# Window attention and top-1 experts on one core: maxima in PSUM, small routing operations on GpSimd, ranks and the early table first in a step, late casts

## The chip, the cores and the metric

The kernel runs on one core of a Trainium2 chip. The core has TensorE (matmuls, into PSUM), VectorE, ScalarE and GpSimd, which work from queues of their own and meet through semaphores, and DMA queues, here those of SyncE and of GpSimd. The metric is the device time of one execution in microseconds (us).

## What is computed

Eight heads of causal attention with a window of 64 over 8 sequences of 576 tokens, and then a mixture of 8 experts in which each token goes to the one expert with the largest logit, weighted by its softmax share. All in float32.

```python
scores = scale * np.matmul(q, k.transpose(0, 1, 3, 2))          # 8 x 8 x 576 x 64
mask = (rel >= 0) & (rel < 64)
scores = np.where(mask, scores, -1e9)
attn = softmax(scores); x = (attn @ v)                           # to 4608 rows of 512
expert_idx = np.argmax(x @ w_gate, axis=1); gate_w = their softmax share
out[mask_e] = gate_w * (np.maximum(x[mask_e] @ w1[e], 0) @ w2[e])   # e = 0..7, F = 1024
```

## The kernel before

**Steps.** The loop at L766 runs 36 attention steps of 128 tokens (NS = 36) and 7 more to drain. A step i is a software pipeline, and the order in which the code calls its parts is the order in each engine's queue: nothing reorders it later. `exps(i-1)` (ScalarE, eight activations `pf`), `evac(i-2)` (ScalarE, `tsb`), `apart(i-2)` (GpSimd, two products `pm` with the mask, L403), `cols_t` (ScalarE, `xT`, L441), then `scores(i)` (TensorE, into `s_b`), `folded` and `largest` (VectorE: fold of the two halves of the window, maximum `mx`, scaled negative maximum `mxs`, L379), `values(i-3)` (TensorE, into `x_b`), one routing matmul (`fast`), `rows_t(i-4)` (TensorE transposes into `m_b` or `t_b`), `transp(i-1)` (TensorE), `shares(i-3)` (VectorE: `den`, `rs`, `xrow`, and the store of the rows by SyncE), and at its end what routing has queued. `scores` alternate between two buffers until step 29 (TURN) and share one from then on. `x_b` also holds the small routing results (`rest_b`) beside the values.

**Routing.** Tokens are routed in four rounds of 8, 6, 12 and 10 tiles. A round's steps s1 to s8 (L489 to L554) go through the queue `slow`, three a step: maxima of logits `lm`, `ld`, `eq`, the exponentials `ex` (L498, ScalarE), the choice `oh`; s4 in the following step (the ranks within each expert: TensorE matmuls with `tri` and `ones`, and ScalarE's copy `rks`, L513), then `pos`, `se`, `g`, `fl`, `mid`, and the parts of the gate in the next. `puts` (L809, four a step) write a one-hot row for each tile (`hot_row`), and after rounds 1 and 2 the tables for two early experts each (`early_parts`, `early_table`, `early_rows`: TensorE gathers, VectorE makes indices `eidx` and gates, GpSimd fetches the tokens `xg`).

**Early experts.** From step 29 the generator `early` (`first_passes`) runs the passes of experts 0 to 3 in pieces between the steps' parts (`forward`, six pieces a step), and after the steps alone. The tokens of expert 0 are transposed in steps 27 and 28 (`turn`, into `m_b`, before the scores). Weights come as float32 and are split in a high part `whi` (ScalarE, L220) and a rest `wlo` (VectorE, L221); `split_ahead` makes one such pair a step from step 29 on, at the step's end, and loads the next by SyncE's queue.

**The plan.** After the steps, `plan` (L636) works out the blocks of the remaining passes on VectorE, a few small operations for every second piece of `early`, and ends in one matmul that spreads `blk` (`diag`, L699); then the table for all later passes, and the passes (`chain`), which fill the time from about 290 us.

## Time and profile before

| | |
|---|---|
| median of 3 runs | 691.14 us (688.66 to 693.12) |
| the profiled execution | 692.4 us, span 690.6 us |
| TensorE busy | 627.2 us, 91% |
| VectorE busy | 424.7 us, 61% |
| ScalarE busy | 359.4 us, 52% |
| GpSimd busy | 193.4 us, 28% |

The span runs from the first to the last instruction of the program. Busy times are those of one engine's instructions; shares over the span mix the attention steps (to about 146 us), the steps with expert pieces between (to about 230 us), the early experts and the plan (to about 290 us) and the later passes. Where an instruction waits, the rows name what ended the idle time.

### The profile page before, as it was taken

To read this page: it belongs to the slowest core of one execution; us is meant where nothing else is said; L and a number is where in the kernel's file an instruction comes from. 1 tells how busy PE (TensorE), PEld (TensorE's weight loads), DVE (VectorE), ACT (ScalarE), POOL (GpSimd) and SP (SyncE) were. 2 spreads that over 40 slices of the span, in tenths; PEclk is the share of its full clock that TensorE was granted. 3 is DMA by queue.
4 is the path that set the end of the run, shared out by engine and by line. 5 is a ranking of instruction groups with operands and counts; after the bars stand their busy time and mean duration, and the time that the engine had idled before them with its cause. 6 is when DMAs were issued, how large, how long until landed. Compare 5 with 4: busy or idle time off the path is not lost.

```text
span 690.6 us, 17098 instructions
## 1 busy us (share of the span) xinstructions
PE 627.2 (91%) x7002; PEld 552.4 (80%) x7002; DVE 424.7 (61%) x817; ACT 359.4 (52%) x760; POOL 193.4 (28%) x159
## 2 busy tenths in 40 slices
PE   5797778678889979999999999999999999999995
PEld 4676666566768768889999999999999999999994
DVE  4687989655676877564544555555565556555651
ACT  4566555644454333553444656555555565555551
POOL 4565545633235103411111212122212212110111
PEclk9999998998999989999999999999999999999999
DMA  9887775854223635854444666666566667555520
GB/s 318 295 261 263 237 280 190 265 182 148 93 88 123 267 122 174 290 206 165 148 168 153 221 216 204 218 227 222 209 219 223 224 217 239 202 193 195 214 92 32
DMA packets 34247, 138.14 MB, mean 200 GB/s; under 512 B 4844, under 2 KB 5996, under 8 KB 24432
## 3 DMA queue, kind: packets, MB, share of 16 engines
q1 hardware_dynamic: 27760, 118.08, 49.3%
q0 software_dynamic: 6400, 18.88, 8.0%
q8 instruction: 57, 0.93, 0.5%
q14 instruction: 30, 0.25, 0.1%
HBM read 119.11 MB, written 19.92 MB: 201 GB/s over the span
## 4 chain that ended last, share of the span: by engine, by line
PE 69%; DVE 14%; ACT 7%; issue 6%; DMA 2%; POOL 0%; DVEq 0%; ACTq 0%; POOLq 0%
PE m_b L279 16%; PE s_b L243 14%; PE t_b L279 13%; PE x_b L243 13%; PE x_b L417 3%; ACT pf L387 3%; PE s_b L361 3%; PE s_b L180 2%; DMA raw<-wall 2%; DVE wlo L221 2%; DVE mx L376 2%; DVE s_b L372 2%; ACT whi L220 2%; DVE mxs L379 1%; DVE xrow L427 1%
## 5 line engine op out<-in xcount | busy, mean ns | idle before, releaser
L221 DVE TENSOR_TENSOR wlo<-raw,whi 128x1024 fp32r<-128x1024 f32 (+1 forms) x158 | 187.2, 1185 | 172.3 <-ACT whi L220 167.9
L220 ACT CAST whi<-raw 128x1024 fp32r<-128x1024 f32 (+1 forms) x158 | 160.9, 1020 | 102.1 <-PE s_b L243 51.1
L403 POOL TENSOR_TENSOR pm<-tsb,cs 128x512 f32<-128x512 f32 x72 | 93.8, 1324 | 109.5 <-ACT tsb L396 106.7
L251 POOL DMA_INDIRECT out<-ys,idx_sb x32 | 40.9, 1277 | 182.9 <-ACT ys L250 178.0
L387 ACT ACTIVATE pf<-s_b,mxs 128x64 f32<-128x64 f32 x288 | 62.7, 333 | 47.8 <-DVE den L423 32.9
L169 POOL DMA_INDIRECT xg<-xs,idx_sb x32 | 34.5, 1080 | 153.4 <-PE s_b L180 140.4
L243 PE MATMUL s_b<-whi,hh 128*128 128x512 f32 x176 | 71.1, 404 | 0.0
L243 PE MATMUL s_b<-whi,hl 128*128 128x512 f32 x176 | 70.1, 398 | 0.6 <-DVE hl L286 0.6
L279 PE MATMUL t_b<-xh,whi 128*128 128x256 f32 (+1 forms) x240 | 70.6, 294 | 0.0
L279 PE MATMUL m_b<-xh,whi 128*128 128x256 f32 (+1 forms) x240 | 70.5, 294 | 0.0
L243 PE MATMUL s_b<-wlo,hh 128*128 128x512 f32 x176 | 70.1, 398 | 0.0
L279 PE MATMUL t_b<-xh,wlo 128*128 128x256 f32 (+1 forms) x240 | 69.7, 291 | 0.0
L279 PE MATMUL m_b<-xh,wlo 128*128 128x256 f32 (+1 forms) x240 | 69.7, 290 | 0.0
L279 PE MATMUL m_b<-xl,whi 128*128 128x256 f32 (+1 forms) x240 | 69.4, 289 | 0.2 <-DVE xl L183 0.2
L279 PE MATMUL t_b<-xl,whi 128*128 128x256 f32 (+1 forms) x240 | 69.4, 289 | 0.0
L285 ACT ACTIVATE hh<-m_b 128x256 fp32r<-128x256 f32 (+1 forms) x82 | 32.5, 397 | 62.0 <-PE m_b L279 61.9
L417 PE MATMUL x_b<-ring,pm 64*64 64x65 f32 x2176 | 47.3, 233 | 16.2 <-issue 6.9
L417 PEld LDWEIGHTS x_b<-ring,pm 64*64 64x64 f32 x2176 | 42.7, 145 | 22.2 <-issue 17.7
L243 PE MATMUL x_b<-wlo,hh 128*128 128x512 f32 x144 | 56.7, 393 | 0.0
L243 PE MATMUL x_b<-whi,hh 128*128 128x512 f32 x144 | 56.5, 393 | 0.0
L243 PE MATMUL x_b<-whi,hl 128*128 128x512 f32 x144 | 56.5, 392 | 0.0
L361 PE MATMUL s_b<-ring 64*64 64x128 f32 x1024 | 43.9, 294 | 8.9 <-ACT pf L387 8.4
(177 smaller groups left out, 1273.7 us busy)
## 6 DMA issues: line engine op xcount, KB each, us to landing
raw<-wall SPq DMA_DIRECT2D x76, 1024.0 KB, 5.0
ring<-qkv SPq DMA_DIRECT2D x66, 386.0 KB, 4.3
xs<-xrow SPq DMA_DIRECT2D x36, 256.0 KB, 2.2
ring<-qkv SPq DMA_DIRECT2D x4, 256.0 KB, 5.2
ring<-qkv SPq DMA_DIRECT2D x4, 130.0 KB, 4.9
ring<-qkv SPq DMA_DIRECT2D x1, 512.0 KB
xg<-xs,idx_sb POOLq DMA_INDIRECT x32, 4.1
out<-ys,idx_sb POOLq DMA_INDIRECT x32, 2.8
```

The costliest lines, as they stand in the source:

```text
L169: nc.gpsimd.indirect_dma_start(out=t[:, u], out_offset=None, in_=xs[0:rows], in_offset=bass.IndirectOffsetOnAxis(ap=ix, axis=0), bounds_ch ...
L180: nc.tensor.transpose(xp[:, kk], t[:, u, kk * P:(kk + 1) * P], ident)
L220: nc.scalar.copy(out=hi[:, s], in_=raw[:, s])
L221: nc.vector.tensor_tensor(out=lo[:, s], in0=raw[:, s], in1=hi[:, s], op=ALU.subtract)
L243: nc.tensor.matmul(y, lhsT=x[:, us], rhs=w[:, C:], start=(j == 0 and m == 0), stop=(j == NJ - 1 and m == 2))
L251: ins = nc.gpsimd.indirect_dma_start(out=out, out_offset=bass.IndirectOffsetOnAxis(ap=ix, axis=0), in_=ys, in_offset=None, bounds_check=N ...
L279: nc.tensor.matmul(hp[:, 0:w], lhsT=a[:, ks], rhs=x[:, kk, 0:w], start=(m == 0), stop=(m == 11))
L285: nc.scalar.activation(out=hh[:, 0:w], in_=hp[:, 0:w], func=AF.Relu)
L361: nc.tensor.matmul(sp[cols, a, g], lhsT=q_r[rows, r, g], rhs=k_r[rows, r - 1:r + 1, g], start=True, stop=True)
L387: nc.scalar.activation(out=pf[:, g, a], in_=sp[:, a, g, 0], func=AF.Exp, bias=mx[:, h:h + 1], scale=SCALE)
L403: nc.gpsimd.tensor_tensor(out=pm[i], in0=t.rearrange("p (g q) -> p g q", g=NG), op=ALU.mult, in1=cc("mask")[:, i * P:(i + 1) * P].unsqueez ...
L417: nc.tensor.matmul(x_b[cols, a, g * V1:(g + 1) * V1], lhsT=pm[i][rows, g, cols], rhs=v_r[rows, c % RING - i, g], start=(i == 0), stop=(i = ...
```

## The change

- `largest` writes the maximum into the score buffer in PSUM, in a half that the fold has done with, and `mxs` is made from there.
- `se` + 1e-9, `fl` and `mid` go from VectorE to GpSimd.
- s4 (ranks) is called first in a step, before `exps`; the early table and the fetches are called there too, one a step from the step after `early_parts` on, in place of spacing by empty `puts`; `puts` are three a step (four after the attention steps).
- `ex` is put behind the next step's `exps`, `evac` and `apart`.
- `cols_t` is called for tile i-4 right after `rows_t(i-4)` in all steps; before step 29 it was called for tile i-5 behind `evac`. The logits keep their step.
- `split_ahead` is called behind `exps` and `evac` of the next step; its `wlo` is made at that step's end.
- `plan` yields three more times between `diag` and its matmul.

```diff
-        mx = wk.tile([P, H], F32, name="mx")
-        nc.vector.tensor_reduce(out=mx, in_=sp_of(n)...[:, :, 0], op=ALU.max, axis=AX.X, negate=True)
+        sp = sp_of(n).rearrange("p a g b w -> p (a g) b w")
+        mx = sp[:, :, 1, 0]
+        nc.vector.tensor_reduce(out=mx, in_=sp[:, :, 0], op=ALU.max, axis=AX.X, negate=True)
...
-            if pieces is None:
+            if lows is not None:
+                nc.scalar.copy(out=hi, in_=raw)
+                lows.append(low)
+            elif pieces is None:
                 piece(slice(0, 2 * C))
...
-            nc.scalar.activation(out=new("ex", E), in_=v["ld"], func=AF.Exp)
+            new("ex", E)
+            exs.append(lambda: nc.scalar.activation(out=v["ex"], in_=v["ld"], func=AF.Exp))
...
-            nc.vector.tensor_scalar(out=v["se"], in0=v["se"], scalar1=1e-9, scalar2=None, op0=ALU.add)
+            nc.gpsimd.tensor_scalar(out=v["se"], in0=v["se"], scalar1=1e-9, scalar2=None, op0=ALU.add)
...
-            nc.vector.tensor_scalar(out=new("fl"), ...
+            nc.gpsimd.tensor_scalar(out=new("fl"), ...
-            nc.vector.tensor_scalar(out=mid[:, ts_], ...
+            nc.gpsimd.tensor_scalar(out=mid[:, ts_], ...
...
-                puts.extend([lambda: early_parts(e0, rows)] + [lambda: None] * 4 + [lambda: early_table(e0, rows)])
-                for e in range(e0, e0 + 2):
-                    puts.extend([lambda e=e: early_rows(e, rows)] + [lambda: None] * 3)
+                puts.append(lambda: early_parts(e0, rows))
+                puts.append(lambda: begin.extend(
+                    (rs_["step"] + 1 + k, f) for k, f in enumerate([lambda: early_table(e0, rows)] + [
+                        lambda e=e: early_rows(e, rows) for e in range(e0, e0 + 2)])))
...
         ts(diag, ident[:, 0:NM], blk, ALU.mult)
+        for _ in range(3):
+            yield
         wp = s_b[0][:, 1, 0:NM]
...
-            w.ready.append(w.split_())
+            w.ready.append(w.split_(lows=lows))
...
+            rs_["step"] = i
+            if slow and slow[0][0]:
+                slow.popleft()[1]()
+            while begin and begin[0][0] <= i:
+                begin.popleft()[1]()
             each(exps, i - 1)
             each(evac, i - 2)
             each(apart, i - 2)
-            if i <= TURN:
-                each(cols_t, i - 5)
+            while exs:
+                exs.popleft()()
+            if i > TURN:
+                split_ahead()
...
-            if rs_["fast"]:
-                rs_["fast"].popleft()()
-            if slow and slow[0][0]:
-                slow.popleft()[1]()
+            if rs_["fast"] and (rs_["fast"][0][0] < i):
+                rs_["fast"].popleft()[1]()
             forward(i, 2)
             each(rows_t, i - 4)
-            if i >= TURN:
-                each(cols_t, i - 4)
+            each(cols_t, i - 4)
...
-            for k in range(4):
+            for k in range(RATE[1] if i < NS else 4):
                 if puts and not slow:
                     puts.popleft()()
-            if i >= TURN:
-                split_ahead()
+            while lows:
+                lows.popleft()()
```

Three places show how the queues move. Line numbers differ between the two kernels. First ScalarE's queue in steps 27 and 28, where expert 0's tokens are transposed into `m_b` (`xeh` is their cast). Before:

```order
L441 COPY xT<-m_b 128x4x128
L182 CAST xeh_106<-m_b 128x4x128
L387 ACTIVATE pf<-s_b_76,mxs 128x64 x8
L396 COPY tsb<-t_b 128x512
L441 COPY xT<-m_b 128x4x128
L182 CAST xeh_106<-m_b 128x4x128
```

and of the change:

```order
L183 CAST xeh_106<-m_b 128x4x128
L449 COPY xT<-m_b 128x4x128
L395 ACTIVATE pf<-s_b_76,mxs 128x64 x8
L404 COPY tsb<-t_b 128x512
L183 CAST xeh_106<-m_b 128x4x128
L449 COPY xT<-m_b 128x4x128
```

The copy `xT`, which empties `m_b`, stood between the exponentials and the cast, and now stands ahead of the exponentials, behind the cast of the step before.

Second ScalarE's queue in steps 31 to 33, around the ranks of the third routing round, with the expert pieces' `hh`. Before:

```order
L498 ACTIVATE ex<-ld 128x96
L220 CAST whi<-raw 128x1024
L387 ACTIVATE pf<-s_b_75,mxs 128x64 x8
L396 COPY tsb<-t_b 128x512
L513 COPY rks<-x_b 128x104
L441 COPY xT<-t_b 128x4x128
L285 ACTIVATE hh<-m_b 128x256
L220 CAST whi<-raw 128x1024
L387 ACTIVATE pf<-s_b_75,mxs 128x64 x8
```

and of the change:

```order
L525 COPY rks<-x_b 128x104
L395 ACTIVATE pf<-s_b_75,mxs 128x64 x8
L404 COPY tsb<-t_b 128x512
L510 ACTIVATE ex<-ld 128x96
L228 CAST whi<-raw 128x1024
L449 COPY xT<-t_b 128x4x128
L292 ACTIVATE hh<-m_b 128x256
L395 ACTIVATE pf<-s_b_75,mxs 128x64 x8
```

`ex` and the cast `whi` moved from ahead of the exponentials `pf` to behind them, and the rank copy `rks` from behind `tsb` to ahead of `pf`.

Third TensorE's queue in step 14, the ranks of the first round. Before, from the transposes `t_b` of step 13 on, up to the values:

```order
L392 MATMUL t_b<-cs_81,pf 128x128 x4
L361 MATMUL s_b_75<-ring 64x128 x16
L417 MATMUL x_b<-ring,pm_1147 64x65 x4
L417 MATMUL x_b<-ring,pm_1148 64x65 x4
```

and of the change:

```order
L400 MATMUL t_b<-cs_81,pf 128x128 x4
L521 LDWEIGHTS tri
L521 MATMUL x_b<-oh,tri 128x72
L523 LDWEIGHTS ones
L523 MATMUL x_b<-oh,ones 128x64
...
L523 LDWEIGHTS ones
L523 MATMUL x_b<-oh,ones 128x8
L368 MATMUL s_b_75<-ring 64x128 x16
```

The nine rank matmuls, which stood behind the values and the logits, now stand ahead of the scores.

## Rows read from the trace of the kernel before

**Rows 1.** The page: busy time of each engine; granted TensorE clock by 40 slices, tenths.

```profile
PE 627.2 (91%) x7002; PEld 552.4 (80%) x7002; DVE 424.7 (61%) x817; ACT 359.4 (52%) x760; POOL 193.4 (28%) x159
PEclk9999998998999989999999999999999999999999
```

**Rows 2.** Busy time by stretch: length, engines (instructions), granted clock, DMA share, GB/s.

```profile
20.00:58.00 38.00, 32.79 (x927) 27.45 (x920) 29.36 (x62) 23.78 (x89) 21.64 (x18) 0.96 0.80 268
146.00:206.00 60.00, 48.93 (x916) 40.12 (x916) 39.52 (x98) 29.35 (x88) 17.33 (x13) 0.94 0.35 120
232.00:290.00 58.00, 51.28 (x320) 45.47 (x321) 42.54 (x112) 22.54 (x37) 15.00 (x12) 0.91 0.53 181
290.00:691.00 401.00, 391.44 (x2438) 354.03 (x2436) 217.26 (x282) 213.77 (x316) 68.55 (x58) 1.00 0.56 192
```

**Rows 3.** By line: busy us, mean ns, idle before; first `mxs` with shortest/median/longest ns.

```profile
L379 DVE TENSOR_SCALAR mxs<-mx x36: 171/231/1192, 8.6 to 199.0; 128x8 f32<-128x8 f32 x36
L379 DVE TENSOR_SCALAR mxs<-mx 128x8 f32<-128x8 f32 x36 | 16.0, 443 | 1.2
L423 DVE TENSOR_SCALAR den<-x_b 128x8 f32<-128x8 f32 x36 | 5.7, 157 | 9.6 <-ACT rks L513 3.3 <-PE x_b L417 2.9 <-PE x_b L476 2.1
L537 DVE TENSOR_SCALAR mid<-fl 128x8 f32<-128x8 f32 (+3 forms) x4 | 3.7, 932 | 0.1
L535 DVE TENSOR_SCALAR fl<-pf 128x8 f32<-128x8 f32 (+3 forms) x4 | 2.7, 685 | 0.0
L403 POOL TENSOR_TENSOR pm<-tsb,cs 128x512 f32<-128x512 f32 x72 | 93.8, 1324 | 109.5 <-ACT tsb L396 106.7 <-PE x_b L417 2.7
L904 POOL MEMSET const-float32-1.0<- 128x1 f32 x1 | 0.1, 105 | 0.0
```

**Rows 4.** Timeline, step 23: start, length, engine, line, operation, count, idle before it.

```profile
110.45 2.86 POOL L403 TENSOR_TENSOR pm<-tsb,cs 128x512 f32<-128x512 f32 x2 [2.44 <-ACT tsb L396]
...
112.32 1.01 DVE L379 TENSOR_SCALAR mxs<-mx 128x8 f32<-128x8 f32 x1
...
113.45 1.75 ACT L387 ACTIVATE pf<-s_b,mxs 128x64 f32<-128x64 f32 x8 [2.29 <-DVE den L423]
```

**Rows 5.** Timeline, steps 13 and 14, around the first round's ranks.

```profile
62.34 1.10 PE L361 MATMUL s_b<-ring 64*64 64x128 f32 x32
...
63.38 0.26 ACT L498 ACTIVATE ex<-ld 128x64 f32<-128x64 f32 x1 [4.68 <-DVE ld L493]
...
63.90 0.22 DVE L504 TENSOR_TENSOR oh<-eq,em 128x64 bf16<-128x64 f32 x1
...
67.32 0.17 DVE L423 TENSOR_SCALAR den<-x_b 128x8 f32<-128x8 f32 x1 [1.67 <-ACT rks L513]
```

**Rows 6.** Timeline, steps 27 to 29: TensorE behind the copy `xT`.

```profile
129.84 0.65 PE L180 MATMUL m_b<-cs,xg 128*128 128x128 f32 x4 [1.58 <-ACT xT L441]
...
136.96 0.66 PE L180 MATMUL m_b<-cs,xg 128*128 128x128 f32 x4 [3.26 <-ACT xT L441]
...
143.99 0.38 PE L279 MATMUL m_b<-xeh,whi 128*128 128x256 f32 x1 [1.24 <-ACT xT L441]
```

**Rows 7.** Timeline, steps 31 and 32: cast, exponentials, scores.

```profile
166.35 1.03 ACT L220 CAST whi<-raw 128x1024 fp32r<-128x1024 f32 x1
167.29 1.74 ACT L387 ACTIVATE pf<-s_b,mxs 128x64 f32<-128x64 f32 x8
...
169.08 1.99 PE L361 MATMUL s_b<-ring 64*64 64x128 f32 x32 [2.95 <-ACT pf L387]
```

**Rows 8.** Waits of the whole span: who for whom, us in total, times, longest.

```profile
PE s_b L361 <- ACT pf L387: 8.4, 6, 3.0
...
PE s_b L699 <- DVE diag L612: 3.3, 1, 3.3
```

**Rows 9.** Timeline, step 23 and its end: the first early table.

```profile
114.55 0.53 PE L580 MATMUL x_b<-said,hot_row 128*128 128x20 bf16 x14 [2.54 <-DVE lgs L462]
...
115.93 1.13 DVE L591 TENSOR_SCALAR eidx<-ix 128x4 int32<-128x4 f32 x1
```

More of the change, by code (lines that the diff above doesn't have):

```diff
@@ L61 @@
 LOADW = 14
+RATE = (3, 3)
 AHEAD = 2
@@ L217, in split_, with low @@
             raw = self.raws[jj][:, r]
+            def low(s=slice(0, 2 * C)):
+                nc.vector.tensor_tensor(out=lo[:, s], in0=raw[:, s], in1=hi[:, s], op=ALU.subtract)
             def piece(s):
                 nc.scalar.copy(out=hi[:, s], in_=raw[:, s])
-                nc.vector.tensor_tensor(out=lo[:, s], in0=raw[:, s], in1=hi[:, s], op=ALU.subtract)
-            if pieces is None:
+                low(s)
+            if lows is not None:
+                nc.scalar.copy(out=hi, in_=raw)
+                lows.append(low)
+            elif pieces is None:
                 piece(slice(0, 2 * C))
@@ L450, in cols_t @@
             args = nt, rs_["lgs"], rs_["tile0"], rs_["round"]
-            rs_["fast"].extend([lambda: logits(xT, lgT), lambda lgs=rs_["lgs"]: by_token(lgT, lgs[:, c0:c0 + 2], args if last else None)])
+            i = rs_["step"]
+            rs_["fast"].extend([(i, lambda: logits(xT, lgT)),
+                                (i, lambda lgs=rs_["lgs"]: by_token(lgT, lgs[:, c0:c0 + 2], args if last else None))])
             if last:
@@ L467, in by_token @@
         rs_["read"] = read
-    slow, puts = deque(), deque()
-    rs_ = {"round": 0, "chunk": 0, "tile0": 0, "fast": deque(), "read": None}
+    slow, puts, begin = deque(), deque(), deque()
+    exs = deque()
+    rs_ = {"step": 0, "round": 0, "chunk": 0, "tile0": 0, "fast": deque(), "read": None}
     def logits(xT, dst):
@@ L534, in s7 @@
             nc.vector.reciprocal(out=new("g"), in_=v["se"])
-            nc.vector.tensor_scalar(out=new("fl"), in0=v["pf2"], scalar1=1.0 / P, scalar2=129.0 / 256,
+            nc.gpsimd.tensor_scalar(out=new("fl"), in0=v["pf2"], scalar1=1.0 / P, scalar2=129.0 / 256,
                                     op0=ALU.mult, op1=ALU.add)
-            nc.vector.tensor_scalar(out=mid[:, ts_], in0=v["fl"], scalar1=RND, scalar2=RND + 1, op0=ALU.add,
+            nc.gpsimd.tensor_scalar(out=mid[:, ts_], in0=v["fl"], scalar1=RND, scalar2=RND + 1, op0=ALU.add,
                                     op1=ALU.subtract)
@@ L734, in each @@
             f(n)
-    pieces = deque()
+    pieces, lows = deque(), deque()
     ew = {}
@@ L805, in window_attention_then_top1_moe @@
                 rs_["read"] = None
-            for k in range(4 if i >= NS else 3):
+            for k in range(RATE[0] if i < NS else 4):
                 if slow and not slow[0][0]:
                     slow.popleft()[1]()
-            for k in range(4):
+            for k in range(RATE[1] if i < NS else 4):
                 if puts and not slow:
                     puts.popleft()()
-            if i >= TURN:
-                split_ahead()
+            while lows:
+                lows.popleft()()
             if pieces:
                 pieces.popleft()()
-        assert not (rs_["fast"] or slow), (len(rs_["fast"]), len(slow))
+        assert not (rs_["fast"] or slow or begin), (len(rs_["fast"]), len(slow), len(begin))
         while puts:
```

4 lines of the change are left out of this document (1 added, 3 removed).

## The prediction

> **What bounds the kernel now.** I read the busy line and the clock line of the page first. TensorE is busy 91% of the span, VectorE 61% [rows 1], but these are averages over stages that differ. So I cut the span into windows [rows 2]. From 290 us on TensorE is busy 391.44 of 401 us at full clock; nothing of that stage is edited, so whatever is won or lost before 290 us should be carried to the end one to one. Ahead of it TensorE is not full: 32.79 of 38 us in the attention steps from 20 to 58 us, 48.93 of 60 us from 146 to 206 us, where attention steps and first expert passes alternate, 51.28 of 58 us from 232 to 290 us. [...] The reader is to see in these rows that only the first 290 us can move, and that its work hangs on hand-overs between TensorE, VectorE, ScalarE and GpSimd.
>
> Then I looked for instructions that last far longer than their size asks. `mxs` takes 171 ns at best, 1192 at worst, 443 in the mean; `den`, of the same 128x8 size but with a PSUM source, takes 157 [rows 3]. The timeline shows why: GpSimd's mask product runs from 110.45 to 113.31, `mxs` starts inside it at 112.32 and ends with it, and the exponentials start right behind [rows 4]. `fl` and `mid`, also small and SBUF to SBUF, average 685 and 932 ns [rows 3]. Last I read who waits: ScalarE and VectorE around a routing round [rows 5], TensorE on the copy `xT` in the steps in which the first expert's tokens are transposed [rows 6], TensorE on the exponentials after step 29 [rows 7, 8], TensorE on the plan's `diag` [rows 8], and the first table [rows 9].
>
> **The change part by part.**
>
> *A, maxima in PSUM.* 36 `mxs` go from 443 to an expected 157 ns, the row of `den`: 36 x 0.286 = 10.3 us of VectorE time. Bounds: nothing, if the time is not tied to the source's place; 10.3 if all of it is on the path. It is not all on the path. From 20 to 58 us TensorE is busy 86% of the time and VectorE 77% [rows 2], so a step can shorten by a seventh at most before TensorE binds; with roughly 20 ordinary steps and stalls in about half of them I take 3.0 us. No wait is added.
>
> [...]
>
> *B, routing.* `fl` and `mid` leave VectorE: 4 x (0.685 + 0.932) = 6.5 us [rows 3]. Two of the four rounds lie in the VectorE-bound steps, where this delays the next `fold`: 3.2 us. The other two lie under TensorE's expert work, counted as nothing (if that cover is gone, 3.2 more). `den` waited 1.67 us for the rank copy `rks` [rows 5]; with ranks first in the step that wait goes, 2 x 1.67 = 3.3. Against this, TensorE now takes up the ranks ahead of the scores, and they need `oh`, ready at 64.12, where the scores started at 62.34 [rows 5]: 1.8 us later in two rounds, -3.6. `g` now waits for `se` from GpSimd. How long a small GpSimd operation lasts no row shows: the bounds are 0.1 us (a memset) and 1.32 (a 128x512 product) [rows 3]; 128x8 is nearest the former, and with two hand-overs I take 0.3 each in two rounds, -0.6. The product of the next step queues behind `mid`, but its users come a step later. `ex` behind the scores' exponentials frees ScalarE, which stood 4.68 us waiting for `ld` [rows 5], but `rks` now stands there and waits for TensorE, so nothing is counted. Three puts a step instead of four stretch them over more steps: nothing. Net 2.3; 2.5 with the shorter queue on VectorE. Bounds -2 and 6.5.
>
> *C, `xT` a step earlier.* In the three steps in which TensorE's first work is the transposing into `m_b` or the first expert matmul there, it waits 1.58, 3.26 and 1.24 us for the copy that empties `m_b`, since that copy stands behind eight exponentials and `tsb` on ScalarE [rows 6]. Moved up to where `m_b` is filled, it is done before. 6.1 us in sum; the cast `xeh` and VectorE's `xel` still read `m_b` before the next rows, so I take 4.0 (bounds 1 and 6.1). The price is a new place: `xT` now stands ahead of the next exponentials and waits for TensorE late in its step; see the rivals.
>
> *D, late casts.* From step 29 on all scores share one buffer, so TensorE's scores wait for the exponentials: six times, 8.4 us [rows 8]. In one of them the chain is `whi` 1.03 us, then the exponentials, then scores after 2.95 us of standing [rows 7]; these 32 scores took 1.99 us where 1.10 is usual [rows 5], as at half clock. With the cast behind, each of five such steps gains 1.03 = 5.2; in the sixth the rank copy takes its place. The halves `wlo` and with them the weights come later by most of a step, which may cost some of it: 4.5 (bounds 1 and 8.4, the whole wait).
>
> *E, early table.* TensorE stood 2.54 us for it at 114.55, and `eidx` took 1.13 us under a product [rows 9]. First in a step, its place no longer waits for that step's logits, but VectorE now waits for TensorE there, and `eidx` can still meet a product: 1.0 (bounds -2 and 2.5).
>
> *F, three more yields* of the plan are six turns of the expert loop ahead of the one matmul that stood 3.3 us for `diag` [rows 8]. TensorE fills that with about nine matmuls and a flush, then meets the `wlo` that VectorE makes in front of `diag`: 2.3 (bounds 0 and 3.3). The table follows six turns later, still ahead of its first fetch, which waits for the early experts anyway.
>
> Sum: 3.0 + 2.5 + 4.0 + 4.5 + 1.0 + 2.3 = 17.3 us. The profiled execution took 692.4 us (span 690.6, and 1.8 around it), 1.3 above the median of 691.1; taken from 692.4 the sum gives 675.1, and set against the median **673.8 us**.
>
> **Rivals.**
>
> *The copy blocks (slower).* In steps 4 to 28 `xT` stands ahead of the next exponentials and waits for TensorE's last work but one. If that ends later than `mxs` by more than the step's slack, ScalarE and TensorE wait in turn. The least wait of that kind now is 1.24 us [rows 6]; 25 steps of it are 31 us: 704.8. It eats the gain up from 17.3 / 25 = 0.69 us a step. Against it: exponentials are next needed by TensorE's transposes at the end of the following step, so two steps lie in the loop.
>
> *Heads of steps stall.* Ranks (4) and tables (2) first in a step make TensorE stand for VectorE. If all six lose 1.8 us more than counted, and three are followed by half-clock scores (+0.9 each): 10.8 + 2.7, 687.3. For it: [rows 5, 7]. Against it: from step 29 on TensorE's own queue is long enough that `oh` is ready earlier.
>
> *Another engine or the transfers bind.* A, B and E free VectorE, but TensorE's share of the steps, or the transfers at 0.80 of their engines from 20 to 58 us [rows 2], may be as close. Then 6.5 us are lost: 680.3.
>
> *The wait moves to other instructions.* GpSimd's 72 products stay, and instructions of VectorE between SBUF operands (`eidx` [rows 9], `hot_row`, the gates) can meet them when the exponentials, and so the products, come earlier. Ten such waits of 0.96 us (1.13 less the best `mxs`) make 683.4. [...]
>
> *More is freed.* If the stretches at half clock go too: (1 - share) x length is 1.5, 3.6 and 5.2 us in the three early windows [rows 2], 10.3 us: 663.5.
>
> **How the numbers follow.** Forecast 0.45 (its own range 667 to 680); more freed 0.13; another bound 0.13; wait moved 0.08; heads of steps 0.12; copy blocks 0.09. One per cent, about what a measurement of this kernel can tell from no change, is 684.2 to 698.0. Faster: 0.45 + 0.13 + 0.13 + 0.08 = 0.79; within: 0.12; slower: 0.09. The range 663 to 687 leaves out the blocking copy and the far ends of two others.
>
> **What would show it.** After: `mxs` near 0.16 us with no spread; no small VectorE operation of 1 us in the rounds; TensorE without waits on `xT` around the first expert's tokens; scores' waits after step 29 down from 8.4 to about 3 us; the plan's matmul without a wait; the last 400 us unchanged in length. I would be wrong if exponentials wait for `xT` in ordinary steps, if TensorE stands at the heads of rank steps with low clock behind, or if `eidx`, `hot_row` and the like grow by what `mxs` lost.

## The result and the profile after

The changed kernel took 683.28 us (median of 8 runs, 681.73 to 686.51) where the kernel before took 691.11 (8 runs, 688.66 to 695.99): a ratio of 0.9877, 95% interval 0.9852 to 0.9901. It is faster, as forecast, and the time lies inside the range; but 7.8 us were won where the sum had 17.3, so the time is 9.5 us above the predicted 673.8. The profiled execution took 684.16 us, span 682.4.

The page of the changed kernel, busy time and granted clock by 40 slices, answers to [rows 1]:

```profile
PE 625.0 (92%) x7002; PEld 551.8 (81%) x7002; DVE 413.8 (61%) x805; ACT 359.5 (53%) x760; POOL 194.9 (29%) x171
PEclk9998986999999999999999999999999999999998
```

Its busy time by stretch, with the columns of [rows 2] (the fourth number from the end is GpSimd's, then the clock):

```profile
20.00:58.00 38.00, 32.83 (x1020) 28.41 (x1020) 26.95 (x66) 24.46 (x90) 21.79 (x18) 1.00 0.85 285
92.00:126.00 34.00, 28.10 (x738) 24.54 (x731) 27.89 (x84) 18.80 (x68) 19.85 (x19) 0.83 0.59 192
232.00:290.00 58.00, 51.54 (x339) 45.38 (x338) 41.18 (x89) 25.34 (x39) 14.72 (x12) 1.00 0.57 204
290.00:682.40 392.40, 383.28 (x2384) 346.66 (x2383) 213.25 (x277) 209.74 (x310) 68.59 (x58) 0.99 0.56 192
```

The granted clock is 1.00 from 20 to 58 and from 232 to 290 us (0.96 and 0.91 in [rows 2]), but there is a new hole: 0.83 from 92 to 126 us, where the kernel before had 0.90. Three more profiles of the same kernel, from the experiments below, agree from 232 to 290 us only (1.00 in all): from 20 to 58 us they have 0.96, 0.96 and 1.00, and from 92 to 126 us 0.93, 0.90 and 0.82. Operations of VectorE, from their own tile's view (count, shortest/median/longest ns, first and last start), in the changed kernel, and the one-hot rows in the kernel before below them:

```profile
L387 DVE TENSOR_SCALAR mxs<-s_b x36: 165/166/167, 8.7 to 192.0; 128x8 f32<-128x8 f32 x36
L570 DVE TENSOR_SCALAR hot_row<-rowb,lo x36: 242/247/1336, 73.4 to 231.1; 128x128 bf16<-128x128 bf16 x36
```

```profile
L557 DVE TENSOR_SCALAR hot_row<-rowb,lo x36: 246/250/255, 75.4 to 237.2; 128x128 bf16<-128x128 bf16 x36
```

The maxima lost their spread (171/231/1192 in [rows 3]), and `hot_row`, which had none, now has one. Waits of TensorE and ScalarE in the changed kernel (total us, times, longest):

```profile
ACT xT L449 <- PE m_b L442: 40.2, 25, 3.9
ACT rks L525 <- PE x_b L523: 10.1, 4, 3.1
PE m_b L286 <- DVE wlo L221: 6.5, 9, 1.1
PE x_b L521 <- DVE oh L516: 5.6, 4, 2.2
PE s_b L368 <- ACT pf L395: 4.3, 5, 1.5
```

The scores' wait for the exponentials is down from 8.4 to 4.3 us and the plan's wait of 3.3 us [rows 8] is gone. New are TensorE's waits for the choice `oh` (the ranks, first in a step), and those for `wlo` in front of `m_b` have grown from 1.2 to 6.5 us.

To see where time went I subtract, for each attention step, the start of its fold on VectorE from that of the kernel before; the last two columns are the last `xrow` and the end of the span. The chip of the result is called chip 0 here; the experiments ran on five, chips 1 to 5, each time beside the kernel before (where an expectation says "call", it means such a chip). The change was profiled four times, and two kernels of the experiments below stand beside it. The kernel before has one profile, with the result, so a lead on another chip also holds the difference between the chips; what a lead gains or loses from one step to the next says more than its height.

| lead over before, us | step 13 | 15 | 22 | 26 | 30 | 32 | 33 | 34 | last xrow | end |
|---|---|---|---|---|---|---|---|---|---|---|
| the change, chip 0 | 1.8 | 2.5 | 1.6 | 2.1 | 6.2 | 6.6 | 10.3 | 6.5 | 7.0 | 8.2 |
| the same, chip 2 | 1.3 | 2.6 | 2.1 | 0.5 | 5.8 | 6.3 | 9.9 | 6.2 | 6.6 | 7.2 |
| the same, chip 4 | 0.1 | 2.3 | 0.0 | 1.3 | 6.5 | 7.0 | 10.6 | 6.8 | 7.4 | 8.9 |
| the same, chip 5 | 0.7 | 2.1 | 0.8 | 0.2 | 2.4 | 2.8 | 6.4 | 2.7 | 3.1 | 4.1 |
| ranks back, chip 5 | 0.9 | 4.7 | 6.0 | 4.9 | 8.0 | 11.8 | 15.0 | 11.3 | 11.8 | 13.9 |
| ranks and copy back, chip 4 | 1.6 | 4.9 | 3.9 | 5.3 | 10.4 | 14.1 | 17.3 | 13.6 | 15.4 | 17.5 |

Up to step 26 the change won 0.2 to 2 us where A, B and E had 6.5 in the sum; steps 26 to 30 gave what C had. Steps 30 to 33 gave 4.1 us, nearly what D had (not all of it is D's, as the late casts below show), but step 34 took 3.7 back, so that from step 30 to the last `xrow` 0.7 to 0.9 is left. In steps 13 to 26 single steps swing by 1 to 2 us from one execution to the next, so only what all four show counts; the gain up to step 33 (4.05 to 4.07) and the loss behind it (3.71 to 3.75) are the same in all four.

### The profile page after: what moved, and what is told of

It reads as the page before. It is cut to its first block, busy times and chain, and to the rows that moved or that the text cites. A ratio compares the mean times of both kernels' runs of the same rounds, so it can differ in the third digit from the quotient of the medians.

```text
span 682.4 us, 17092 instructions
## 1 busy us (share of the span) xinstructions
PE 625.0 (92%) x7002; PEld 551.8 (81%) x7002; DVE 413.8 (61%) x805; ACT 359.5 (53%) x760; POOL 194.9 (29%) x171
## 4 chain that ended last, share of the span: by engine, by line
PE 73%; DVE 13%; issue 6%; ACT 4%; POOL 2%; DMA 1%; POOLq 0%; DVEq 0%; ACTq 0%
PE m_b L286 16%; PE x_b L250 14%; PE s_b L250 14%; PE t_b L286 13%; PE x_b L425 5%; PE s_b L368 3%; ACT pf L395 2%; PE s_b L181 2%; DVE wlo L221 2%; DVE xrow L435 1%; PE x_b L487 1%; POOL pm L411 1%; DVE s_b L385 1%; DMA ring<-qkv 1%; DVE s_b L379 1%
## 5 line engine op out<-in xcount | busy, mean ns | idle before, releaser
L224 ACT CAST whi<-raw 128x1024 fp32r<-128x1024 f32 (+1 forms) x147 | 149.1, 1015 | 102.1 <-PE s_b L250 51.3
L411 POOL TENSOR_TENSOR pm<-tsb,cs 128x512 f32<-128x512 f32 x72 | 91.2, 1288 | 93.5 <-ACT tsb L404 85.2
L425 PE MATMUL x_b<-ring,pm 64*64 64x65 f32 x2176 | 49.0, 233 | 14.4 <-issue 4.8
L425 PEld LDWEIGHTS x_b<-ring,pm 64*64 64x64 f32 x2176 | 43.8, 145 | 19.9 <-issue 15.4
L293 DVE SCALAR_TENSOR_TENSOR hl<-m_b,hh 128x256 fp32r<-128x256 f32 (+1 forms) x82 | 35.4, 432 | 25.0 <-ACT hh L292 24.9
```

The source lines that it names most:

```text
L224: nc.scalar.copy(out=hi[:, s], in_=raw[:, s])
L293: nc.vector.scalar_tensor_tensor(out=hl[:, 0:w], in0=hp[:, 0:w], scalar=0.0, in1=hh[:, 0:w], op0=ALU.max, op1=ALU.subtract)
L411: nc.gpsimd.tensor_tensor(out=pm[i], in0=t.rearrange("p (g q) -> p g q", g=NG), op=ALU.mult, in1=cc("mask")[:, i * P:(i + 1) * P].unsqueez ...
L425: nc.tensor.matmul(x_b[cols, a, g * V1:(g + 1) * V1], lhsT=pm[i][rows, g, cols], rhs=v_r[rows, c % RING - i, g], start=(i == 0), stop=(i = ...
```

## Experiments

The median of the kernel before differs between the chips, 691 to 698 us, and ratios of one kernel differ by 0.1 to 0.6%. Where a few us decide, kernels on one chip are compared.

| kernel (chip) | median us, range | before us | ratio, 95% interval |
|---|---|---|---|
| before + maxima in PSUM (1) | 693.75, 689.06 to 696.11 | 696.38 | 0.9938, 0.9912 to 0.9964 |
| before + early copy (1) | 689.54, 687.40 to 691.83 | 696.38 | 0.9907, 0.9877 to 0.9937 |
| change, copy back (1) | 682.23, 679.17 to 686.04 | 696.38 | 0.9801, 0.9765 to 0.9838 |
| change, ranks back (1) | 679.23, 676.75 to 682.63 | 696.38 | 0.9749, 0.9711 to 0.9786 |
| change again (2) | 685.44, 683.46 to 690.22 | 695.11 | 0.9859, 0.9824 to 0.9895 |
| change, copy and ranks back (2) | 677.19, 676.11 to 679.65 | 695.11 | 0.9737, 0.9707 to 0.9767 |
| change, one-hot rows on GpSimd (2) | 681.23, 679.72 to 685.66 | 695.11 | 0.9799, 0.9766 to 0.9833 |
| change, casts back (2) | 684.51, 683.80 to 688.50 | 695.11 | 0.9854, 0.9821 to 0.9887 |
| copy, ranks back, rows on GpSimd (3) | 675.97, 673.61 to 677.98 | 698.38 | 0.9666, 0.9633 to 0.9700 |
| copy, ranks, casts back (3) | 676.07, 675.08 to 678.89 | 698.38 | 0.9680, 0.9645 to 0.9714 |
| copy, ranks back, small ones on VectorE (3) | 683.39, 682.55 to 685.78 | 698.38 | 0.9788, 0.9754 to 0.9822 |
| change without yields (3) | 688.68, 685.60 to 689.50 | 698.38 | 0.9847, 0.9811 to 0.9882 |
| change, third time (4) | 681.93, 680.80 to 683.92 | 693.62 | 0.9837, 0.9801 to 0.9874 |
| change without yields (4) | 686.88, 683.07 to 691.07 | 693.62 | 0.9907, 0.9872 to 0.9942 |
| copy and ranks back (4) | 675.72, 674.48 to 677.21 | 693.62 | 0.9750, 0.9714 to 0.9785 |
| the same, rows on GpSimd, casts back (4) | 674.89, 671.97 to 679.03 | 693.62 | 0.9736, 0.9692 to 0.9781 |
| change, fourth time (5) | 686.31, 682.22 to 689.38 | 695.80 | 0.9845, 0.9798 to 0.9893 |
| change, ranks back (5) | 678.64, 676.74 to 682.80 | 695.80 | 0.9761, 0.9717 to 0.9805 |

### Two parts alone

In the kernel before, only the maxima:

```diff
-        mx = wk.tile([P, H], F32, name="mx")
+        mx = sp[:, :, 1, 0]
```

> The kernel before with one part of the change alone: the maximum is written into the score buffer in PSUM, and the scaled maximum is made from there; the queues are untouched. The changed kernel shows the scaled maximum at about 0.17 us each without spread, and still only 2 us of lead at step 26, where 6.5 had been forecast for maxima, routing and table together. Theory 'swallowed': the maxima are worth what was forecast or more (3 to 5 us by step 26), and other parts of the change gave it back in the same steps. Then this kernel takes 686 to 688 us, 0.993 to 0.995 of before, and its folds lead before's by 3 to 5 us at step 26. Rival 'never on the path': VectorE's locked time was slack, TensorE or a transfer bound these steps. Then 690 to 691 us and a lead under 1 us at step 26.

0.9938 is 4.3 us (2.5 to 6.1): the maxima do what was forecast, or a little more. The fold leads by 2.7 us at step 25. (The profiled execution, 696.11 us, was the slowest of the twelve, and lost that lead behind step 25.)

In the kernel before, only the copy:

```diff
-            if i <= TURN:
-                each(cols_t, i - 5)
...
-            if i >= TURN:
-                each(cols_t, i - 4)
+            each(cols_t, i - 4)
```

> The kernel before with one part of the change alone: the copy xT of the rows of tile i-4 right behind their transposes in every step, where it stood behind the next step's tsb before step 29; the logits keep their step. Theory 'swallowed': in steps 4 to 26 the copy makes the exponentials wait for TensorE, and this costs 1 to 3 us there even beside the slow maxima of before, while in steps 27 to 29 TensorE's three waits for xT (6.1 us) go and about 4 are kept. Net 687 to 690 us, the lead of the folds below zero at step 26 and up by 4 from there to step 30. Rival 'harmless': no loss before step 26, 4 us won behind it, 687 us or a little less, lead about zero at step 26.

6.5 us won, more than either theory had, with a lead of 4.6 at step 26: alone, the early copy costs the ordinary steps nothing. TensorE's waits for `xT` from 126 to 146 us fell from 6.0 to 0.7 us, as they did in the change.

### The new places put back

The copy, in the change (behind `apart` again up to step 26, and in its new place from there on):

```diff
             each(apart, i - 2)
+            if i <= TURN - 3:
+                each(cols_t, i - 5)
...
-            each(cols_t, i - 4)
+            if i >= TURN - 3:
+                each(cols_t, i - 4)
```

> The changed kernel with the copy xT back behind tsb of the next step in steps 5 to 26 (at step 26 both the copy of the old place and that of the new one are made), and in the new place from step 26 on. The changed kernel shows 25 idle times of ScalarE in front of this copy, 40 us in sum, most of them idle time that had been spent elsewhere. Theory 'swallowed by the copy': those in front of exponentials whose maxima are ready cost 2 to 4 us by step 26; then 679 to 681 us, and the lead over before at step 26 rises from 2 to 4 to 6 us. Rival 'slack': the loop spans two steps and the waits hid in it; then 682.5 to 684 us and a lead that stays near 2.

The ranks, in the change:

```diff
-            if slow and slow[0][0]:
-                slow.popleft()[1]()
             while begin and begin[0][0] <= i:
...
                 rs_["fast"].popleft()[1]()
+            if slow and slow[0][0]:
+                slow.popleft()[1]()
```

> The changed kernel with the ranks back in their old place behind the values and the logits, and the rank copy behind them; the rest is the change. The changed kernel loses 2.4 us of its lead at step 14 and 2.5 at step 20, where TensorE stands 1.8 and 2.2 us for the choice oh, and wins most of it back in the step behind, where VectorE no longer waits for the rank copy. Theory 'heads of steps': the stalls cost 1 us a round more than they save, 2 to 3 us in all with half-clock work behind them; then 680.5 to 682 us. Rival 'a swap': what is lost at the head is saved at the copy; then 682.7 to 684 us, and the lead at step 22 stays between 1 and 3 us.

Both gained, the ranks more. But with the copy back the leads up to step 19 are those of the change (3.8 against 3.2 and 3.5); they part at step 22 only (5.4 against 1.6 and 2.1). So the copy did not block step by step. (These are the leads on chips 0 and 2; chips 4 and 5 have 1.3 and 1.9 at step 19, 0.0 and 0.8 at step 22.) Both edits together, with the change itself on the same chip:

> The changed kernel itself, so that it stands on the same chip beside the runs that follow; before took 696.4 us on the chip of the first four experiments and 691.1 in the first comparison. By its first ratio, 0.9877, it takes 683 us where before takes 691 and 688 where before takes 696. If the ranks' place is the main loss ('heads of steps'), it is some 6 to 9 us slower than the kernel with the ranks in the old place on one chip, and its profile again shows the loss of lead at steps 14, 20 and 22; if the first comparison was off or the loss at step 22 was chance, it comes within 3 us of that kernel and step 22 keeps its lead.

> The changed kernel with both put back: the copy xT in its old place before step 26, and the ranks in their old place. Ratios to before so far: 0.9877 for the change, 0.980 with the copy back, 0.975 with the ranks back. Theory 'two separate losses': the gains add, and the ratio is 0.966 to 0.971 (5 us less than with the ranks alone). Rival 'one loss, two ways out': both put back mend the same thing, the jam of TensorE, VectorE's one-hot rows and GpSimd's products around steps 20 to 22, and together they bring no more than the ranks alone: 0.973 to 0.977.

0.9737 is the ratio with the ranks alone back (0.9749) within the intervals: the copy's old place mends nothing that the ranks' old place does not mend as well. Two further chips had each of these kernels beside the change.

> The changed kernel again, as the base of this call. Ratios so far 0.9877 and 0.9859; expected 0.984 to 0.988, with the same loss of lead at step 22 in its profile.

> The changed kernel with the copy xT and the ranks in their old places, a second time, beside the change on one chip. Theory 'the new places cost what is missing': 7 to 9 us below the change in this call. If the earlier difference came from the chips, it is 3 to 5 us.

> The changed kernel as the base of this call: ratio 0.983 to 0.988 (so far 0.9877, 0.9859 and 0.9837).

> The changed kernel with the ranks alone in their old place, beside the change on one chip. Theory 'the ranks first in a step are the loss': 5 to 8 us below the change in this call, nearly all of the 6.2 us by which both places together stood below it. Rival 'half and half': 2.5 to 4.5 us below it, and the copy has the other half.

681.93 against 675.72: 6.2 us for both, a little less than expected. 686.31 against 678.64: 7.7 us for the ranks alone by the medians, 6.5 by the means of the six runs of each (3 to 10). About 7 us is what the runs support. The ranks' place is the loss; the copy's place adds nothing that these runs can tell. Where it arises, the timelines show, that of the first profile of the change beside that of the kernel with the ranks back on chip 5. The change around the first round's ranks:

```profile
60.17 0.58 ACT L449 COPY xT<-m_b 128x512 f32<-128x512 f32 x1 [2.18 <-PE m_b L442]
...
62.06 0.23 DVE L516 TENSOR_TENSOR oh<-eq,em 128x64 bf16<-128x64 f32 x1
62.34 0.19 PE L521 MATMUL x_b<-oh,tri 128*128 128x72 bf16 x1 [1.76 <-DVE oh L516]
...
62.65 1.90 PE L368 MATMUL s_b<-ring 64*64 64x128 f32 x32
62.76 0.22 ACT L525 COPY rks<-x_b 128x72 f32<-128x72 f32 x1 [2.00 <-PE x_b L523]
62.87 1.75 ACT L395 ACTIVATE pf<-s_b,mxs 128x64 f32<-128x64 f32 x8
64.31 1.98 PE L425 MATMUL x_b<-ring,pm 64*64 64x65 f32 x64
```

and with the ranks back in their old place:

```profile
60.63 1.10 PE L368 MATMUL s_b<-ring 64*64 64x128 f32 x32
60.78 1.75 ACT L395 ACTIVATE pf<-s_b,mxs 128x64 f32<-128x64 f32 x8
...
61.55 1.11 PE L425 MATMUL x_b<-ring,pm 64*64 64x65 f32 x64
...
62.31 0.23 DVE L516 TENSOR_TENSOR oh<-eq,em 128x64 bf16<-128x64 f32 x1
...
64.11 0.21 PE L521 MATMUL x_b<-oh,tri 128*128 128x72 bf16 x1
```

`oh` is ready at nearly the same time, 62.29 and 62.54. In the old place TensorE fills the time until then with scores and values. In the new one three things happen: TensorE stands 1.76 us; the exponentials, whose maxima were ready at 59.15, stand behind `xT` and `rks` until 62.87; and the scores and values behind the stall run 1.90 and 1.98 us instead of 1.10 and 1.11, at a granted clock of 0.50 from 62.8 to 66.2 us. By step 15 the two kernels on chip 5 are 2.7 us apart. The third round, in step 32, repeats it: the scores wait 1.52 us for exponentials that stood behind `rks`, and the gap between the two grows from 5.7 us at step 30 to 9.0 at step 32.

Between them lies step 22, where the gap on chip 5 grows by 2.4 us. These three places make up nearly all of the 8.7 us between the two kernels at the last `xrow`; in the second round, step 20, the change loses 2.1 us and has them back a step later. The timeline of the change at step 22:

```profile
100.47 0.64 ACT L404 COPY tsb<-t_b 128x512 f32<-128x512 f32 x1
...
101.03 2.73 DVE L570 TENSOR_SCALAR hot_row<-rowb,lo 128x128 bf16<-128x128 bf16 x3
101.19 2.52 POOL L411 TENSOR_TENSOR pm<-tsb,cs 128x512 f32<-128x512 f32 x2 [0.80 <-ACT tsb L404]
...
106.33 0.15 DVE L431 TENSOR_SCALAR den<-x_b 128x8 f32<-128x8 f32 x1
...
107.37 0.41 DVE L488 COPY lgT<-x_b 128x256 f32<-128x256 f32 x1
...
107.92 0.88 PE L425 MATMUL x_b<-ring,pm 64*64 64x65 f32 x21 [3.80 <-DVE lgT L488]
```

and with the ranks back:

```profile
98.77 0.58 DVE L570 TENSOR_SCALAR hot_row<-rowb,lo 128x128 bf16<-128x128 bf16 x3
...
99.24 0.64 ACT L404 COPY tsb<-t_b 128x512 f32<-128x512 f32 x1
...
99.96 2.51 POOL L411 TENSOR_TENSOR pm<-tsb,cs 128x512 f32<-128x512 f32 x2 [1.83 <-ACT tsb L404]
...
103.52 0.70 PE L425 MATMUL x_b<-ring,pm 64*64 64x65 f32 x32 [1.61 <-DVE lgT L488]
```

Three one-hot rows take 0.58 us when they start 1.19 us ahead of GpSimd's product, and 2.73 us when they start 0.16 ahead, so that two of them, of 1.32 us each, meet its two products. The fold, `den` and `lgT` queue behind them on VectorE, and TensorE stands 3.80 us instead of 1.61. All four profiles of the change have this jam, with a stall of 3.80 or 3.81 us; no profile with copy or ranks back has it. The hole in the clock from 92 to 126 us is deeper than before's 0.90 in two of the four only (0.83 and 0.82); with the ranks back it is 0.91. Why the ranks' place shifts VectorE against GpSimd by just that much was not taken apart.

### The one-hot rows themselves

```diff
-            nc.vector.tensor_scalar(out=hot_row[:, t0 + t], in0=rowb, ...
+            nc.gpsimd.tensor_scalar(out=hot_row[:, t0 + t], in0=rowb, ...
```

> The changed kernel with the 36 one-hot rows made by GpSimd instead of VectorE, so that they can't meet its products from another engine. In the profile of the change four of these rows lasted 0.6 to 1.3 us each beside a product, two of them ahead of step 22, behind which TensorE stood 3.8 us and then ran 2 us of scores at half clock. Theory 'the wait moved to the one-hot rows': without it 2 to 4 us are won, 679 to 681 us where the change takes 683 (0.982 to 0.985). Rival: GpSimd's rows queue ahead of its products, and a row of 128x128 lies between its 0.27 us for 128x8 and 1.32 for 128x512; three of 0.4 to 0.6 us a step push the products back by more than a us in a dozen steps, and the time is the same or up to 5 us longer (0.987 to 0.995).

4.2 us faster than the change on its chip, so the rows' stalls cost time. But step 22 is not the whole of it. Against the change on the same chip the folds of this kernel gain 2.6 us at step 22, where the stall of 3.81 us is gone, and have lost 2.0 of that by step 27 (TensorE stands 2.38 us for the first early table instead of 1.15); they gain 2.6 us a second time at step 34, where the change loses 3.7 and this kernel 1.1, and 1.8 behind the last `xrow`. The second jam is shown under the late casts. GpSimd takes longer for a row, 605 ns at the median where VectorE takes 247 in the change, as the tile's view of that kernel shows:

```profile
L570 POOL TENSOR_SCALAR hot_row<-rowb,lo x36: 592/605/1624, 73.3 to 232.1; 128x128 bf16<-128x128 bf16 x36
```

In the kernel with copy and ranks back the same edit has no jam at step 22 to end:

> The changed kernel with the copy xT and the ranks in their old places, and the one-hot rows on GpSimd as well. Ratios so far: 0.9859 for the change on the chip of the second call, 0.9737 with copy and ranks back, 0.9799 with the one-hot rows on GpSimd. Theory 'two jams': copy and ranks in the old place end the jam of the one-hot rows at step 22, but the one behind step 33 (rows of 1.3 us beside products, the lead down by 3.7 us there) is still in that kernel, and in the run with the rows on GpSimd the lead fell by 1.1 us there only. Then 2 to 3 us more are won: 0.969 to 0.971. Rival: the rows cost GpSimd 0.6 us each and push the products of the third and fourth round's steps back by as much as they free; then no gain, 0.973 to 0.977.

675.97 us is what the kernel without this edit took on two other chips (677.19 and 675.72), though the ratio is lower, 0.9666, since before was at its slowest there (698.38). I count it as no gain, but no chip had it beside the kernel without the edit, so the point stays open. Its profile shows both sides: the folds lose 1.1 us at step 34 instead of 3.7, and TensorE stands 4.43 us for the first early table, whose parts come later, where it is 1.88 us with the rows on VectorE.

### The late casts

```diff
-            if i > TURN:
-                split_ahead()
...
-            while lows:
-                lows.popleft()()
+            if i >= TURN:
+                split_ahead()
```

and `split_()` without `lows`, in the change and then in the kernel with copy and ranks back:

> The changed kernel with the weights' pair made at the step's end again, cast and rest together, ahead of the next exponentials (as before the change). The change had been counted at 4.5 us there; its profile shows TensorE's waits for the exponentials down from 8.4 to 4.3 us but a lead that grew by only 0.8 us from step 30 to step 35, with new waits of TensorE for wlo. Theory 'the wait moved to wlo': the late cast is worth 0 to 1.5 us, and this kernel takes the time of the change within 1.5 us (0.986 to 0.990). Rival 'the late cast paid as forecast, and something else ate it': 3 to 5 us slower than the change (0.992 to 0.995), and its lead at step 35 is smaller than at step 30 by 3 us or more.

> The changed kernel with copy, ranks and also the weights' pair (cast and rest) in the old place. In the changed kernel the late cast was worth nothing (0.9854 without it, 0.9859 with it). Theory 'given back': the cast's 1 us a step is won in the steps and lost behind them, since wlo is made a step later and TensorE meets it; then this kernel takes the same as with the late cast, 0.9737 within 0.002. Rival 'hidden by the jam': in the freer kernel the late cast pays what was forecast, and this kernel is 3 to 5 us slower, 0.978 to 0.981.

684.51 against 685.44, and 676.07 us where the kernel with the late casts took 677.19 and 675.72 on other chips: nothing either way. It is a gain and two losses. From step 28 to step 33 the folds gain 7.2 us on before with the late casts and 4.7 without, so the late casts are worth 2.5 there. TensorE's waits from 146 to 232 us show the exchange. With the casts in the old place, in the change:

```profile
PE s_b L368 <- ACT pf L395: 7.0, 6, 1.9
PE t_b L442 <- DVE xel L184: 1.4, 1, 1.4
```

and in the change with late casts:

```profile
PE s_b L368 <- ACT pf L395: 3.2, 4, 1.5
PE t_b L442 <- DVE xel L184: 3.2, 2, 1.8
PE m_b L286 <- DVE wlo L221: 3.1, 4, 1.1
```

What leaves the exponentials (3.8 us) comes back on `wlo` and on `xel`, which stands behind it on VectorE (4.9). The longer of the two waits for `xel` is the first loss, and it is the one-hot rows again. In step 33 of the change, on chip 2:

```profile
179.19 2.51 POOL L411 TENSOR_TENSOR pm<-tsb,cs 128x512 f32<-128x512 f32 x2 [3.14 <-ACT tsb L404]
179.24 1.27 DVE L559 TENSOR_TENSOR val<-g,val 128x12 bf16<-128x12 f32 x1
...
180.42 1.66 DVE L570 TENSOR_SCALAR hot_row<-rowb,lo 128x128 bf16<-128x128 bf16 x3
...
185.40 1.09 PE L442 MATMUL t_b<-cs,xrow 128*128 128x128 f32 x4 [1.75 <-DVE xel L184]
```

and with the casts in the old place, on the same chip:

```profile
182.74 0.19 DVE L559 TENSOR_TENSOR val<-g,val 128x12 bf16<-128x12 f32 x1
182.83 0.57 DVE L570 TENSOR_SCALAR hot_row<-rowb,lo 128x128 bf16<-128x128 bf16 x3
...
183.62 3.29 POOL L411 TENSOR_TENSOR pm<-tsb,cs 128x512 f32<-128x512 f32 x2 [3.65 <-ACT tsb L404]
```

With the cast out of their way the exponentials and `tsb` come earlier, and so do GpSimd's products: they now start ahead of the gate's `val` and the rows and stretch both, by 1.1 us each, and `wlo`, the fold and `xel` queue behind. The folds lose 3.7 us at step 34 in every profile with late casts and rows on VectorE, with the ranks in either place (5.9 with the small operations on VectorE too). They lose 1.1 to 1.2 with the casts in the old place or the rows on GpSimd: 2.6 us are the jam's. Second, behind the steps, from the start of the last `xrow` to the end of the last store, late casts cost 1.1 to 2.0 us: 465.1 to 466.0 us in four profiles against 464.0, and 464.6 twice against 462.6. Casts back and rows on GpSimd together:

> As the kernel before it in this call, and with the one-hot rows on GpSimd and the weights' casts in the old place as well. Each of the two alone gave about the same time as that kernel (0.967 and 0.968 on a third chip). Theory 'nothing more to win there': within 1.5 us of the kernel before it. Rival 'they add': 2 to 5 us below it, which would make the late cast a loss and the rows' jam behind step 33 a loss that is left.

674.89 against 675.72: nothing more. This kernel and the two with one of the edits are the fastest of all, level with the plain one with copy and ranks back: 2.5 to 3.3% below before, and 1% below the change. Late casts with the products of step 33 held back behind the rows were not tried.

### The small operations

```diff
-            nc.gpsimd.tensor_scalar(out=v["se"], ...
+            nc.vector.tensor_scalar(out=v["se"], ...
```

likewise `fl` and `mid`, in the kernel with copy and ranks back:

> The changed kernel with copy and ranks in the old place, and the three small operations of a round (se with 1e-9, fl, mid) on VectorE again. The prediction counted 6.5 us of VectorE's time for fl and mid, half of it on the path, less 0.6 for hand-overs: 2.6 us. Theory 'as forecast': 2 to 3.5 us slower than with them on GpSimd, 0.9765 to 0.9787, with fl and mid of up to 1.3 us beside products. Rival 'small': their stalls lie in places of slack or do not come back at this phase, and the time is the same within 1.5 us, 0.9716 to 0.9758.

683.39 us. By the ratios, 0.9788 against 0.9737 and 0.9750 on other chips, the three are worth 2.6 to 3.5 us on GpSimd; against the two other kernels on its own chip, which have them there and differ by one more edit each that was worth nothing elsewhere, 7.3 to 7.4. The folds show 3.4 to 5.0: from step 32 to 35 they lose 4.6 us with the three on VectorE, and lose 1.2 or gain 0.4 in the two profiles with them on GpSimd. So 3 us at the least, and likely more. The place was not the expected one. The timeline in step 32:

```profile
166.54 2.50 POOL L411 TENSOR_TENSOR pm<-tsb,cs 128x512 f32<-128x512 f32 x2 [4.71 <-ACT tsb L404]
166.57 1.27 DVE L535 TENSOR_TENSOR base<-base,cs 128x8 f32<-128x8 f32 x1
...
167.93 1.23 DVE L539 TENSOR_TENSOR pos<-pos,oh 128x96 f32<-128x96 f32 x1
...
171.04 0.58 PE L286 MATMUL m_b<-xeh,wlo 128*128 128x256 f32 x1 [3.46 <-DVE wlo L221]
```

`fl` and `mid` take 0.16 and 0.17 us here. But nothing stands ahead of the products on GpSimd, so they start into VectorE's routing; with the three on GpSimd they queue behind `mid`, and `base` and `pos` take 0.17 and 0.25 us. So part of the gain of moving them seems to be that they hold the products back; no run separates it from the rest.

### The yields

```diff
-        for _ in range(3):
-            yield
```

> The changed kernel without the three more yields of the plan. The forecast counted 2.3 us for them; in the profile of the change the wait of 3.3 us for diag is gone, and the stretch behind the last attention rows became 1.2 us shorter. Theory 'half of the wait': this kernel is 1 to 2.5 us slower than the change (0.9859 on the second chip): 0.987 to 0.990, with TensorE again standing 2 to 3.5 us for diag. Rival 'nothing': TensorE then meets wlo or the table instead, and the time is the same within 0.7 us.

> The changed kernel without the three more yields of the plan, a second time, beside the change on one chip. Its profile showed the wait of 3.3 us for diag again, and a stretch behind the last attention rows about 2 us longer than with the yields, but its ratio (0.9847) was not above that of the change. Theory 'two thirds of the wait': 1 to 2.5 us slower than the change in this call. Rival 'nothing': within 0.7 us of it.

Without them TensorE stands for `diag` as before, in the second of these:

```profile
PE s_b L712 <- DVE diag L625: 3.3, 1, 3.3
```

From the last `xrow` to the last store it is 467.5 and 468.7 us, against 465.1 to 466.0 in four profiles with them: 2.6 us. The medians do not agree as well: 4.9 us on the chip that has both (runs from 683 to 691), and no difference by the ratio on the other chip. The stretch is the better measure, since the steps ahead of it swing.

## Why the prediction was half right

The direction was right, the size was not: 7.8 us where the sum had 17.3. The step that failed first is the ranks' new place in B, counted at -0.3 us and measured at about -7. The second is D, counted at 4.5, of which nothing is left.

**A, maxima in PSUM: right.** All 36 last 165 to 167 ns, below even the best from SBUF (171 [rows 3]), and alone they are worth 4.3 us (3.0 forecast).

**B, routing: the step that failed.** "1.8 us later in two rounds, -3.6", set off against 3.3 saved on `rks`, made the ranks' new place worth -0.3. It cost about 7 (7.7 by the medians on chip 5). The wait for `oh` was sized well (1.76, 2.2 and 1.28 us); what was left out is all that hangs on it. "but `rks` now stands there and waits for TensorE, so nothing is counted" is where it went wrong: the exponentials stand behind `rks`. D even says of one of its steps that in it "the rank copy takes its place", and prices nothing for that. The scores after the stalls of the first two rounds took 1.90 us each where 1.10 is usual, at a granted clock of 0.50 from 62.8 to 66.2 and from 90.1 to 93.4 us, which the rival had in and the sum did not; after that of the third they took 1.10, at 1.00. The third round was taken as covered by the expert pieces, "TensorE's own queue is long enough that `oh` is ready earlier": it stood 1.28 us for `oh` and 1.52 for the exponentials, and 3.3 us were lost. And the shift let the one-hot rows meet the products at step 22, 2.4 us on chip 5. The small operations, counted at 2.6, were worth 3 to 7, in part, as it seems, by holding the products back, which no sentence had.

**C, the early copy: right.** The waits went (6.0 to 0.7 us) and steps 26 to 30 gave 4.1 us in the first profile, 2.1 to 5.4 in the others.

**D, late casts: mechanism right, gain wrong.** The exponentials' waits fell from 8.4 to 4.3, and up to step 33 the late casts are worth 2.5 us. "which may cost some of it" names one loss, `wlo` a step later: 1.1 to 2.0 us behind the steps. The other is not in the sum: earlier exponentials bring earlier products, which met `val` and the one-hot rows of step 33 and cost 2.6. That is the rival of the moved wait, in a place of its own.

**E** was not tried by itself. The first table's stall of 2.54 us [rows 9] is 0.55 to 1.15 in the four profiles of the change, now behind `said`, but 1.9 with the ranks back; what of it is the table's own place stays open. Nor was the slower rate of the `puts`, counted as nothing, tried by itself, though it sets when the one-hot rows run. **F: right**, 2.6 by the stretch for 2.3.

So the sum of 17.3 was reached, by other terms, once the ranks stand where they stood: 17.2 us on chip 5 (695.80 to 678.64) and 17.9 on chip 4 with the copy back too (693.62 to 675.72). There A, C and the small operations paid more than their terms, and D nothing, since the jam of step 33 is in both. That they come out at the forecast's number is luck.

Of the rivals, **heads of steps stall** is what happened, at about 7 of the 13.5 us that it priced; its argument against itself, the long queue after step 29, did not hold. **The wait moves to other instructions** named `hot_row` and came true in two places: 2.4 to 2.6 us at step 22, which belong to the ranks' place, and 2.6 at step 34, which belong to the late casts. The run that takes the rows off VectorE won 4.2 of them; ten waits of 0.96 had been priced. A one-hot row took 1.32 us beside GpSimd's products, which are 1.26 each, and 0.25 without. By what means a product holds a row up, no run shows. **The copy blocks** fell: ScalarE's 25 waits of 40.2 us in sum look alarming and cost nothing that could be measured, alone (6.5 us won) or once the ranks are back; with the ranks first, the copy's place has a part in the jam of step 22. **Another engine binds** is not supported, since the same kernel went about 7 us faster with one part of a step moved. **More is freed** is half there: in all four profiles the granted clock rose to 1.00 from 232 to 290 us and to 0.97 from 146 to 206 us, from 20 to 58 us in two of them only, and in two a new hole opened at 92 to 126 us (0.83 and 0.82). The half clock of which the prediction speaks is in the trace of before as a granted clock of 0.50, from 169 to 175 and from 234 to 237 us.

## What to carry to other kernels

Before work is called first in a step, ask of each of its hand-overs what is ready then, and list what stands behind it on every queue that it enters; the price of a wait at a queue's head was here the wait (1.76 us for `oh` in the first round), plus all that queued behind (exponentials whose maxima were ready at 59.15 began at 62.87), plus, in the first two rounds, slower matmuls after it (1.90 us of scores instead of 1.10). A large idle sum in front of an instruction says little: 40 us before the copy cost nothing that could be measured with the ranks in mid-step, 5.6 us before the ranks went with a loss of about 7. When an operation that lasted longer beside another engine's is taken away (`mxs`, 1192 ns at the longest [rows 3], then 167), or the other engine's is made to come earlier, look at who stands beside that one next: here the one-hot rows, 255 ns at the longest before and 1336 in the change. And follow the lead step by step: D's gain and its loss cancel in the total, and only steps 33 and 34 show them.

## What was not expected of the hardware

GpSimd's operations could be the long ones too. Its `fl`, 0.20 us at the shortest, took 1.21 when VectorE's `wlo` of 1.16 had begun 0.01 us earlier, and ended 0.06 us behind it; timeline of the change:

```profile
171.65 1.16 DVE L221 TENSOR_TENSOR wlo<-raw,whi 128x1024 fp32r<-128x1024 f32 x1
171.66 1.21 POOL L547 TENSOR_SCALAR fl<-pf 128x12 f32<-128x12 f32 x1 [0.19 <-DVE pf L545]
```

Three one-hot rows took 2.73 us where the first started 0.16 us ahead of a product, and 0.58 where it started 1.19 ahead. Such a jam can repeat nearly exactly, 3.80 or 3.81 us in each of four profiles at step 22 and 3.71 to 3.75 us of lead lost in each at step 34, while other steps swing by 1 to 2 us. The kernel before varied between chips by 1% (medians 691.1 to 698.4 us), the change by 0.6% (681.9 to 686.3), and not in step, so that the ratios of one kernel on two chips differ by up to 0.6% without a cause in the kernels.
